# The order in which float64 weights are narrowed: blocks 4 to 7 of the first layer

## The chip, the cores and the metric

The kernel runs on one core of a Trainium2 chip. The metric is the device time in microseconds (us) of one execution, as the median of several runs. A separate profiled execution gives the trace from which durations are taken.

The core has five engines with a queue each: TensorE (PE in the profile; its weight loads are PEld), VectorE (DVE), ScalarE (ACT), GpSimd (POOL) and SyncE (SP, which here issues most of the transfers). Each engine works through its own queue in order and waits on semaphores for what other engines or transfers deliver.

## The reference

Two layers follow each other. The first is a state-space layer (Mamba2 SSD) over `x` of 4 x 8 x 768 x 32, computed in chunks of 32; its output, brought to 3072 tokens of 256 features, goes through a feed-forward block:

```python
h = x @ w_in                                # 3072 x 256 by 256 x 2048
g = h * (1.0 / (1.0 + np.exp(-1.702 * h)))  # quick GELU
return (g @ w_out).astype(np.float32)       # 2048 x 256
```

Inside a chunk the first layer needs decays `exp(cum_i - cum_j)`, a causal product of C and B weighted by them, and a state carried from chunk to chunk. The weights `w_in` and `w_out` come as float64.

## The kernel before

**Tiling.** The 3072 tokens are worked in 6 groups of 512. The 2048 hidden features are 16 blocks of 128 (f = 0 to 15), and each block's weights are two tiles of 128 x 128. For group 0 the hidden layer is a plain product: `hidden(0, f)` issues the matmuls of block f into a PSUM bank (line 895; TensorE's queue holds them as four matmul rows of 128 x 512 per block) and a SiLU on ScalarE (line 898). There are four such banks, used in turn, so block f needs block f-4's SiLU done. Later groups use a scheme with seven products in place of eight (`first`, `product`), with sums of blocks prepared on VectorE.

**Narrowing the weights.** The kernel loads the 64-bit words as pairs of 32-bit words and builds float32 from the fields. This goes in pieces (`PIECES`): pieces 0 to 3 hold two blocks of `w_in` each (0-1, 2-3, 4-5, 6-7), pieces 4 and 5 four blocks each (8-11, 12-15), and pieces 6 to 9 are `w_out`. For each piece:

- `fetch(i)` (line 180): SyncE issues two transfers.
- `fields(i)`, the first step (lines 192 and 195): VectorE cuts out the exponent (tile p) and the mantissa (tile m) of the high words.
- `clamp(i)` (lines 203 and 204): ScalarE turns the exponent field, in place, into that of a float32.
- `rounded(i)` (line 208): VectorE adds the low words to the mantissa.
- `join(i, parts)`, the last step (lines 222 and 228): VectorE puts the sign to the exponent and multiplies by the mantissa; the result is the piece's part of `w_in` or `w_out`. With `parts=2` it does this in two halves of the columns, each with its own two instructions, so that the first blocks are usable before the last. The joins of pieces 1 and 5 also issue a later fetch.

`narrow(i)` does `rounded(i)`, `join(i)` and `fields(i + 1)`, in an order that depends on i.

**Order.** The order on every engine is that of the program text (`in_order` at the end fixes it). For group 0 the loop over f runs `hidden(0, f)` and then what `in_hidden[0]` lists for that f:

```python
for i, k, c in ((2, 1, 1), (3, 2, 2), (4, 4, 7), (5, 8, 11), (6, 11, 14), (7, 14, 15)):
    at(in_hidden[0], k, lambda i=i: narrow(i))
    at(in_hidden[0], c, lambda i=i: clamp(i + 1))
```

So `narrow(2)` and the clamp of piece 3 come after block 1, `narrow(3)` and the clamp of piece 4 after block 2, `narrow(4)` after block 4, the clamp of piece 5 after block 7. `join(0, 2)`, `join(1)`, `fields(2)` and `clamp(2)` come before the loop.

**What else lies there.** After block 5, SyncE's queue holds the store of the decays, further fetches and loads. After block 8, `pick_a` (line 369, ScalarE) makes X from the clipped decays `az`; after block 9, `fan_all` (line 415, TensorE) spreads X over the partitions into ab, and VectorE scans it into the decays L (line 453). After block 15 group 0's second product starts (line 992, tiles o), with the narrowing of `w_out` beside it. Ahead of block 9 of that second product come the scores cb (line 685), the product A (line 716, `gain`), and CsT (line 670, `since_start`), which VectorE makes from the transposed C in the PSUM bank that A's second tile uses after it.

Of the kernel before, what the change touches and what calls it, by code (L numbers as in the profile page):

```python
# [35 lines left out]
def kernel(  # L36
# [126 lines left out]
    def fetch(i, held=False):  # L163
        name, f, n = PIECES[i]
        if n == 2 and f % 4:
            t = pieces.pop(i - 1)[:, 2 * n * DM:]
        else:
            t = pieces[i] = words(f"bits{i}")
            t = t[:, :2 * n * DM]
        if held:  # L170
            held.memset(t[:, :1], 0)
        if name == "in":
            src = moe_w_in[:, 2 * f * P:2 * (f + n) * P].rearrange("(k p) e -> p k e", p=P)
            dst, src = (v.rearrange(s, h=n, e=2 * P) for v, s in (
                (t, "p (h k e) -> k p h e"), (src, "p k (h e) -> k p h e")))
        else:
            src = moe_w_out[f * P:(f + n) * P, :].rearrange("(f p) (h e) -> h p f e", p=P, h=2)
            dst = t.rearrange("p (h f e) -> h p f e", h=2, f=n)
        for k in range(2):
            nc.sync.dma_start(out=dst[k], in_=src[k])  # L180
        t = t.rearrange("p (e w) -> p e w", w=2)
        bits[i] = t[:, :, 0], t[:, :, 1]
# [5 lines left out]
    def fields(i):  # L188
        hi, cols = bits[i][1], slice(0, PIECES[i][2] * DM)
        mantissa[i] = wide.tile([P, PN], U32, tag="m", name=f"m{i}")[:, cols]  # L190
        power[i] = wide.tile([P, PN], U32, tag="p2", name=f"p2{i}")[:, cols]
        nc.vector.tensor_scalar(out=power[i], in0=hi, scalar1=0x7FF00000, scalar2=None,
                                op0=ALU.bitwise_and)

        nc.vector.tensor_scalar(out=mantissa[i], in0=hi, scalar1=0x000FFFFF,
                                scalar2=0x00100000, op0=ALU.bitwise_and, op1=ALU.bitwise_or)
# [9 lines left out]
    def rounded(i):  # L206

        nc.vector.scalar_tensor_tensor(out=mantissa[i].bitcast(FP32), in0=bits[i][0],
                                       scalar=2.0 ** -32, in1=mantissa[i],
                                       op0=ALU.mult, op1=ALU.add)  # L210
# [4 lines left out]
    def join(i, parts=1):  # L215

        name, f, n = PIECES[i]
        n //= parts
        low, m, p2 = bits.pop(i)[1], mantissa.pop(i), power.pop(i)
        for k in range(parts):  # L220
            cols, fs = slice(k * n * DM, (k + 1) * n * DM), slice(f + k * n, f + (k + 1) * n)
            nc.vector.scalar_tensor_tensor(out=p2[:, cols], in0=low[:, cols], scalar=0x80000000,  # L222
                                           in1=p2[:, cols], op0=ALU.bitwise_and, op1=ALU.bitwise_or)
            if name == "in":
                dst, h = w_in[:, fs].rearrange("p f k e -> p (f k e)").unsqueeze(1), 1
            else:
                dst, h = w_out[:, :, fs].rearrange("p c f e -> p c (f e)"), 2
            nc.vector.scalar_tensor_tensor(  # L228
                out=dst, in0=m[:, cols].bitcast(FP32).rearrange("p (h e) -> p h e", h=h),
                scalar=2.0 ** -20, in1=p2[:, cols].bitcast(FP32).rearrange("p (h e) -> p h e", h=h),  # L230
                op0=ALU.mult, op1=ALU.mult)
        for n in NEXT.get(i, ()):
            fetch(n)

    def narrow(i):
        rounded(i)
        if i in (4, 5):
            join(i, 2)
        if i + 1 < len(PIECES):
            fields(i + 1)  # L240
        if i not in (4, 5):
            join(i)


    scratch = dram.tile([NC, 2, NB * NH, H], FP32, name="scratch")
# [989 lines left out]
# [3 lines that stand above are left out]
# [6 lines left out]
    at(in_project[0], 2, lambda: decay(PG + 1), lambda: clip_rows(1),  # L1244
       lambda: decay_rows(1), lambda: turn(PG + 1))
    at(in_project[0], 5, lambda: narrow(9))
    at(in_project[0], 9, lambda: score(pairs), lambda: gain(pairs), lambda: keep_both(pairs, True),
       lambda: weigh(PG), lambda: weigh(PG + 1))
# [201 lines left out]
```

## Time and profile before

| what | value |
|---|---|
| runs: median (lowest to highest) | 349.3 us (348.98 to 349.34) |
| profiled execution: its own time | 350.67 us |
| profiled execution: span from first to last instruction | 348.8 us |
| granted TensorE clock, mean | 1.000 |
| TensorE busy | 341.6 us |
| VectorE busy | 254.6 us |
| ScalarE busy | 155.0 us |
| HBM traffic over the span | 73 GB/s |

A row of the timeline has the start in us, the duration in us, engine, line, operation, tiles out<-in, shape, and the number of instructions merged in it; brackets at its end give idle time of that engine just before and what ended it. In a list of waits the three numbers are the total in us, the number of times, and the longest. Idle time of an engine that nobody waits for costs nothing. Ends of matmuls are modelled.

### The profile page before, as it was taken

Reading aid. Unit: us, or ns where it says so; the run is one execution under the profiler, and the core shown is the slowest. Engines: PE = TensorE matmul, PEld = TensorE weight load, DVE = VectorE, ACT = ScalarE, POOL = GpSimd, SP = SyncE. Lnnn points to the kernel's source line nnn. Section 1 sums busy time; section 2 is a strip of 40 time slices with the busy share of each in tenths; the row PEclk is TensorE's granted clock in tenths of the full one; section 3 lists DMA queues with packets and bytes.
Section 4 is the critical chain, followed back from the end, with each engine's and each line's share of the span. In section 5 each row is a group of like instructions: output and inputs, shape, how many; then the busy total and the mean of one; then the engine's idle time right before and its main releaser. Section 6 shows DMA issues by size and latency. Waiting matters only on the chain.

```text
span 348.8 us, 8124 instructions
## 1 busy us (share of the span) xinstructions
PE 341.6 (98%) x3380; PEld 268.9 (77%) x3380; DVE 254.6 (73%) x481; ACT 155.0 (44%) x352; POOL 13.1 (4%) x42
## 2 busy tenths in 40 slices
PE   8989999999999999999999999999999999999996
PEld 6634444445688888888888888888888888899996
DVE  5889997999878999667997467788465654465463
ACT  4797585205453322654432554332564331554320
POOL 8300000100000100000000000000000000000000
PEclk9999999999999999999999999999999999999999
DMA  6599889624627200415704027400000300000301
GB/s 158 134 300 213 189 181 245 113 54 105 113 49 131 66 0 2 75 57 124 123 18 63 0 59 130 73 1 2 0 4 3 55 7 0 0 2 0 62 0 61
DMA packets 89980, 25.92 MB, mean 74 GB/s; under 512 B 73432, under 2 KB 87128, under 8 KB 89944
## 3 DMA queue, kind: packets, MB, share of 16 engines
q1 hardware_dynamic: 89112, 24.88, 33.5%
q10 hardware_dynamic: 832, 0.52, 0.5%
q8 instruction: 26, 0.43, 0.5%
q14 instruction: 10, 0.08, 0.1%
HBM read 22.15 MB, written 3.24 MB: 73 GB/s over the span
## 4 chain that ended last, share of the span: by engine, by line
PE 90%; DMA 3%; DVE 2%; SPq 1%; ACT 1%; issue 1%; ACTq 1%; POOL 0%; DVEq 0%
PE acc L1055 28%; PE X L950 19%; PE Y L960 14%; PE o L992 8%; PE acc L1062 7%; PE h L895 5%; DMA bits<-in_moe_w_in_dram 3%; PE y L839 2%; PE cb L685 2%; PE y L825 1%; SPq L180 1%; PE A L716 1%; PE ab L557 1%; DMA zC<-in_C_dram 1%; DVE p L222 1%
## 5 line engine op out<-in xcount | busy, mean ns | idle before, releaser
L955 ACT ACTIVATE ac<-X 128x256 f32<-128x256 f32 x76 | 29.1, 383 | 81.5 <-PE X L950 80.7
L1082 DVE TENSOR_TENSOR gT<-Y,ac 128x512 f32<-128x512 f32 x38 | 26.2, 689 | 40.1 <-PE Y L960 32.5
L1055 PE MATMUL acc<-mg,mw 128*128 128x256 f32 x192 | 54.5, 379 | 0.0
L927 ACT ACTIVATE gT<-gT 128x512 f32<-128x512 f32 (+1 forms) x76 | 38.9, 518 | 29.0 <-DVE gT L1082 28.5
L950 PE MATMUL X<-my,mi 128*128 128x256 f32 x152 | 45.1, 380 | 0.0
L1055 PEld LDWEIGHTS acc<-mg,mw 128*128 128x128 f32 x192 | 36.5, 190 | 5.0
L895 PE MATMUL h<-yT,w_in 128*128 128x512 f32 x80 | 35.6, 598 | 1.1 <-DVE w_in L228 0.6
L1082 DVE TENSOR_TENSOR gT<-Y,b 128x256 f32<-128x256 f32 x38 | 15.9, 419 | 28.5 <-PE Y L960 28.5
L1055 PE MATMUL acc<-gT,w_out 128*128 128x256 f32 x128 | 35.5, 379 | 0.0
L950 PEld LDWEIGHTS X<-my,mi 128*128 128x128 f32 x152 | 28.0, 190 | 3.9 <-ACT ac L955 0.2
L895 PEld LDWEIGHTS h<-yT,w_in 128*128 128x128 f32 x80 | 14.7, 190 | 19.7 <-issue 15.9
L992 PE MATMUL o<-gT,w_out 128*128 128x512 f32 x64 | 28.3, 595 | 0.0
L918 DVE TENSOR_TENSOR mg<-gT 128x512 f32<-128x512 f32 x40 | 27.2, 681 | 0.0
L1055 PEld LDWEIGHTS acc<-gT,w_out 128*128 128x128 f32 x128 | 24.2, 190 | 3.4 <-ACT yT L873 0.2
L955 ACT ACTIVATE b<-X 128x256 f32<-128x256 f32 x38 | 14.6, 383 | 21.2 <-PE X L950 20.7
L950 PE MATMUL X<-yT,w_in 128*128 128x256 f32 x76 | 23.2, 389 | 0.0
L960 PE MATMUL Y<-yT,w_in 128*128 128x256 f32 x76 | 22.7, 381 | 0.0
L960 PE MATMUL Y<-my,mi 128*128 128x256 f32 x76 | 22.7, 380 | 0.0
L960 PE MATMUL Y<-yT,mi 128*128 128x256 f32 x76 | 22.5, 379 | 0.0
L950 PE MATMUL X<-my,w_in 128*128 128x256 f32 x76 | 22.5, 379 | 0.0
L992 PEld LDWEIGHTS o<-gT,w_out 128*128 128x128 f32 x64 | 11.8, 190 | 13.6 <-issue 13.4
L405 DVE TENSOR_TENSOR_SCAN L<-a,idents 128x1024 f32<-128x1024 f32 x9 | 20.5, 2277 | 0.2 <-DMA a<-scratch 0.2
(159 smaller groups left out, 546.9 us busy)
## 6 DMA issues: line engine op xcount, KB each, us to landing
a<-scratch SPq DMA_DIRECT2D x18, 256.0 KB, 4.8
bits<-in_moe_w_out_dram SPq DMA_DIRECT2D x8, 512.0 KB, 6.6
x<-in_x_dram SPq DMA_DIRECT2D x24, 128.0 KB, 3.1
out_dram<-ob SPq DMA_DIRECT2D x40, 64.0 KB, 1.9
bits<-in_moe_w_in_dram SPq DMA_DIRECT2D x8, 256.0 KB, 4.4
bits<-in_moe_w_in_dram SPq DMA_DIRECT2D x4, 512.0 KB, 11.9
b<-in_B_dram SPq DMA_DIRECT2D x20, 64.0 KB, 2.6
af<-in_a_dram SPq DMA_DIRECT2D x3, 384.0 KB
```

What stands on the lines that cost most here:

```text
L405: nc.vector.tensor_tensor_scan(out=L, data0=ra[p].rearrange("p k e -> p (k e)"), data1=idents.rearrange("p h i -> p (h i)"), initial=0.0, ...
L685: nc.tensor.matmul(out=s["cb"][side, r, k].rearrange("p (q i) -> p q i", q=Q), lhsT=BT[rows, k, side], rhs=CT[rows, k, :, side], start=Tru ...
L895: nc.tensor.matmul(out=h, lhsT=w_in[:, f, k], rhs=yT[g][:, k], start=(k == 0), stop=(k == NK - 1), skip_group_check=True)
L918: nc.vector.tensor_tensor(out=t[:, 0:2], in0=B[:, :, 1], in1=B[:, 0], op=ALU.subtract)
L927: nc.scalar.activation(o, i, AF.Silu, scale=GELU_SCALE)
L950: nc.tensor.matmul(out=s["X"], lhsT=lhsT, rhs=rhs, start=i == "1", stop=i == "4", skip_group_check=True)
L955: nc.scalar.activation(copy, s["X"], AF.Copy)
L960: nc.tensor.matmul(out=o, lhsT=lhsT, rhs=rhs, start=s.pop("new", False), stop=i != "5", skip_group_check=True)
L992: nc.tensor.matmul(out=o[c], lhsT=w_out[:, c, f], rhs=gT[g, f // 2][:, f % 2], start=(f == 0), stop=(f == NF - 1), skip_group_check=True)
L1055: nc.tensor.matmul(out=acc[g][0][i][:, cols], lhsT=w, rhs=h[:, cols], start=(j == 0 and k == 0 and (i, 0) in begins), stop=(j == NF // 2 - ...
L1062: nc.tensor.matmul(out=o[k] if type(o) is list else o[:, cols], lhsT=h[:, cols], rhs=w, start=(j == 0 and (i, k) in begins), stop=(j == NF ...
L1082: nc.vector.tensor_tensor(out=o, in0=v, in1=w, op=ALU.add)
```

## The change

Two things change in `narrow`. For piece 2 (blocks 4 and 5) the last step is put ahead of the first step on piece 3 (blocks 6 and 7). For piece 3 the last step stays behind the first step on piece 4, but works on one block at a time: two pairs of instructions on 256 columns each instead of one pair on 512.

```diff
     def narrow(i):
         rounded(i)
-        if i in (4, 5):
-            join(i, 2)
+        if i in (2, 4, 5):
+            join(i, 1 if i == 2 else 2)
         if i + 1 < len(PIECES):
             fields(i + 1)
-        if i not in (4, 5):
-            join(i)
+        if i not in (2, 4, 5):
+            join(i, 2 if i == 3 else 1)
```

On VectorE the queue from the rounding of piece 2 to the rounding of piece 4 becomes (before on the left):

```
rounded(2)             rounded(2)
fields(3)              join(2)            2 instructions, 128x512
join(2)                fields(3)
rounded(3)             rounded(3)
fields(4)              fields(4)
join(3)                join(3) block 6    2 instructions, 128x256
                       join(3) block 7    2 instructions, 128x256
rounded(4)             rounded(4)
```

The order on the other engines' queues is the same as before; VectorE has two instructions more.

## The prediction

> **What bounds the kernel now.** I read the page's first two parts, then PE's waits, then each engine's timeline between 15 and 68 us, where the weights are prepared. Page:
> ```profile
> span 348.8 us, 8124 instructions
> PE 341.6 (98%) x3380; PEld 268.9 (77%) x3380; DVE 254.6 (73%) x481; ACT 155.0 (44%) x352; POOL 13.1 (4%) x42
> ```
> PE is busy in 98% of the span. So a change off PE counts only where it moves one of PE's few idle stretches. PE's waits from 17 to 68.5 us (who, whom, total, times, longest):
> ```profile
> PE ab L415 <- ACT X L369: 0.8, 1, 0.8
> PE h L895 <- DVE w_in L228: 0.6, 1, 0.6
> PE A L716 <- DVE CsT L670: 0.3, 1, 0.3
> ```
> From 68.5 to 348 us the same view lists no wait at all: what comes after 68.5 us follows PE's own stream. The three waits in PE's timeline:
> ```profile
> 26.18 10.57 PE L895 MATMUL h<-yT,w_in 128*128 128x512 f32 x24 [0.63 <-DVE w_in L228]
> ...
> 37.59 0.69 PE L415 MATMUL ab<-X,ones 32*64 32x256 f32 x16 [0.84 <-ACT X L369]
> ...
> 67.53 0.70 PE L716 MATMUL A<-x,Be 64*32 64x64 f32 x47 [0.31 <-DVE CsT L670]
> ```
> The first is the matmul of block 4, held by the join of piece 2 (blocks 4, 5). The second is the fan-out of X, which ScalarE makes. The third is the gate that matters: everything later hangs on 67.53. VectorE:
> ```profile
> 17.02 0.42 DVE L222 SCALAR_TENSOR_TENSOR p<-bits,p 128x256 uint32<-128x256 uint32 x1
> 17.47 0.42 DVE L228 SCALAR_TENSOR_TENSOR w_in<-m,p 128x256 f32<-128x256 f32 x1
> ...
> 23.94 0.43 DVE L192 TENSOR_SCALAR p<-bits 128x512 uint32<-128x512 uint32 x1 [0.75 <-DMA bits<-in_moe_w_in_dram]
> ...
> 24.62 0.69 DVE L222 SCALAR_TENSOR_TENSOR p<-bits,p 128x512 uint32<-128x512 uint32 x1
> 25.34 0.69 DVE L228 SCALAR_TENSOR_TENSOR w_in<-m,p 128x512 f32<-128x512 f32 x1
> ...
> 26.87 0.69 DVE L192 TENSOR_SCALAR p<-bits 128x1024 uint32<-128x1024 uint32 x1 [0.24 <-DMA bits<-in_moe_w_in_dram]
> ...
> 28.80 0.69 DVE L228 SCALAR_TENSOR_TENSOR w_in<-m,p 128x512 f32<-128x512 f32 x1
> 29.41 1.22 DVE L208 SCALAR_TENSOR_TENSOR m<-bits,m 128x1024 f32<-128x1024 uint32 x1
> ...
> 33.21 0.69 DVE L192 TENSOR_SCALAR p<-bits 128x1024 uint32<-128x1024 uint32 x1
> ...
> 57.72 0.69 DVE L192 TENSOR_SCALAR p<-bits 128x1024 uint32<-128x1024 uint32 x1 [1.77 <-DMA bits<-in_moe_w_out_dram]
> ...
> 67.04 0.42 DVE L670 TENSOR_TENSOR CsT<-tp,since 128x256 f32<-128x256 f32 x1
> ```
> VectorE waits for transfers at 23.94, 26.87 and 57.72. The last wait is 1.77 long, and from there VectorE's chain of scans leads to CsT at 67.04, whose end releases A. So the gate hangs on a transfer, not on the steps that are moved. ScalarE:
> ```profile
> 25.89 0.58 ACT L898 ACTIVATE gT<-h 128x512 f32<-128x512 f32 x1
> 27.60 1.15 ACT L203 ACTIVATE p<-p,edge 128x1024 f32<-128x1024 uint32 x1 [1.14 <-DVE p L192]
> ...
> 33.93 1.15 ACT L203 ACTIVATE p<-p,edge 128x1024 f32<-128x1024 uint32 x1
> ```
> ScalarE has 1.14 us idle before the clamp of piece 4. The clamp of piece 5 starts 0.03 after VectorE's p (33.21 + 0.69 = 33.90): VectorE sets it.
>
> **The change, part by part.** Neither moved step issues a transfer (a join fetches only for pieces 1 and 5), and neither passes anything on SyncE's or GpSimd's queue; only VectorE's order changes.
>
> *Join of piece 2 first.* Its first instruction needs ScalarE's clamp of piece 2, whose second half runs 22.92 to 23.64. At 20.38 such an instruction started 0.04 after its clamp, so the join starts at 23.69 instead of 24.62. It takes 0.72 to the second instruction and 0.69 more: weights ready at 25.10, not 26.03. VectorE idled for the transfer until 23.94 anyway, so this new wait (0.5) costs nothing: its cover is that idle, 0.75. PE started 0.15 after the weights; 25.25 is earlier than PE's next free slot (26.18 less 0.63 idle less the 0.16 by which matmuls of 0.59 overlap at a pitch of 0.43: 25.39). Block 4 starts at 25.39, **0.79 earlier**, and the first wait is gone.
>
> *First step of piece 3 later.* Its p starts 0.61 after the join's last instruction, at 25.02, not 23.94: 1.08 later. Queued behind are m, rounding of piece 3 (25.81 to 26.50, before 25.95 to 26.64), and then piece 4's first step, which waits for its transfer until 26.87 as before. ScalarE waits for that p: clamp of piece 3 at 25.48 and 26.23, not 24.51 and 25.26; behind it the SiLU of block 2 moves from 25.89 to 26.86. ScalarE can start the next 0.48 later, at 27.34, before 27.60: the 1.14 idle hides it with 0.26 to spare. Without that cover it would cost up to 0.97.
>
> *Join of piece 3 in two halves.* The pair of 512 columns takes 28.09 to 29.41, 1.32. Pairs of 256, from the join of piece 0, go 16.22, 16.68, 17.02, 17.47, 17.81: 1.59 for both. So **VectorE loses 0.27**. Block 6 is ready at 28.97, not 29.50; block 7 at 29.76, 0.26 later, but PE needs it only at 30.84. PE reaches block 6 at 25.39 + 8 x 0.43 = 28.83, waits until 29.12, and runs blocks 6 to 9 some 0.53 earlier than before (29.65). Block 8's weights (31.96 + 0.27 + 0.15 = 32.38) still precede their slot at 32.56.
>
> The row says 0.27. [...]
>
> *What is late next.* Nothing on VectorE waits for a transfer between 26.87 and 33.21, so rounding and join of piece 4 and the first step of piece 5 all come 0.27 later: p at 33.48. ScalarE's clamp of piece 5 goes from 33.93 to 34.20, the SiLU of block 8 behind it to 36.43, X to 36.91, and the fan-out ab from 37.59 to 37.86. PE gets there 0.53 early and waits about 1.6 instead of 0.84. **The gain of 0.53 is eaten by the second wait, and PE leaves it 0.27 late.** From there PE runs without a gap to 66.92, so it comes to A 0.27 late. A waits for CsT, 0.31 before; 0.04 of that stays. VectorE's own 0.27 vanishes in its waits of 0.33 at 45.43 and 1.77 at 57.72. The transfer behind the latter was issued at 50.14 in a SyncE queue that waits for older transfers, not for these joins (its buffer is free at about 39).
>
> **Sum**: -0.79 (block 4) + 0.26 (block 6's new wait) + 0.53 (given back at ab) + 0.27 (ab later) - 0.27 (taken up at A) = **0.0 us** on the span of 348.8. The profiled execution took 350.67, 1.87 outside the span, unchanged. It lies 1.4 above the median of the runs, 349.3, to which I apply the 0.0: **349.3**. Bounds of the unknown: less than nothing only if PE's 0.53 survived both ab and A (-0.53); more if A's slack were missing (+0.27). I take 0, since 0.27 lies under 0.31, though narrowly.
>
> **The rivals.**
> *The delay goes through.* If in unprofiled runs the transfer for 57.72 lands earlier, A's wait is shorter and up to 0.27 shows: 349.6. For it: the runs are 1.4 shorter than the profiled one. Against: a DMA share of 0.99 from 50 to 57.6 us.
> *The gain goes through.* If ab were not set by VectorE's p and A not by CsT, 348.8. For it: removing a wait on the busiest engine. Against: 33.90 to 33.93, and 67.53. Both would have to be wrong.
> *Slower: the cover of the early join goes.* If the transfers for pieces 3 and 4 land early, the old order does piece 3's first step while the clamp of piece 2 runs (23.11 to 23.79), and loses nothing; the new one idles on VectorE from 23.11 to 23.69. Piece 4's first step could be at 25.73 in the old order and 26.42 in the new: 0.69, and 0.27 for the halves: 0.96, 350.3. It begins to count when piece 4's transfer lands before 26.4, and decides the sign at 0.2% when it lands about 0.45 before that and CsT's transfer early too. Against: DMA shares of 0.93 and 1.09 from 18 to 32 us.
> *Slower: PE's clock.* PE's idle stretch at ab doubles. The granted clock is 1.00 in every window, even 0 to 6 us with PE busy 4.64 of 6.00; from 32 to 38 it would now be busy about 4.4. Each matmul at twice its pitch would cost 0.43, so three of them pass 0.7: 350.5 or more. [...]
>
> **How the numbers follow.** No change 0.71; delay through 0.13; gain through 0.05; cover gone 0.09; clock 0.02. About 0.2% (0.7 us) is what a measurement of this kernel can tell from no change. The first two lie inside it and the third mostly; with scatter between runs (348.98 to 349.34 already) I give faster 0.05, same 0.84, slower 0.11. The range goes from the gain (348.8, less 0.1 scatter) to nearly the lost cover: 348.7 to 350.1.
>
> **What the profile after would show.** Right: no wait of h on w_in near 25.4; a wait of about 0.3 before block 6; ab near 37.86 after an idle of about 1.6; A still near 67.5 after almost none. Wrong: ab earlier than 37.5, ScalarE's clamp of piece 4 after 27.7, A moved, or a clock under 1.00.

## The result, and the profile after

The changed kernel takes 351.29 us (median of 20 runs, 349.66 to 352.87) against 349.19 us before (20 runs, 348.44 to 350.40). The ratio is 1.0051, with a 95% interval of 1.0036 to 1.0066: **slower by half a per cent**, about 1.8 us by the ratio (the medians lie 2.1 apart). The forecast was no change, 349.3 us, with a range up to 350.1. It was wrong.

The 20 runs after the change are of two kinds, by the TensorE clock that was granted. Nine have a mean clock of 0.999 or 1.000 and a median of 350.18 us; eleven have 0.994 or 0.995 and a median of 351.71 us. So there are two costs to explain: about 1.0 us in every run (0.8 in a second set of runs, below), and 1.5 us more in about half of them.

The profile shown here is of a run at 0.999 (349.66 us). The head of the page of the changed kernel, and TensorE's waits from 17 to 68.5 us:

```profile
span 347.7 us, 8127 instructions
PE 341.0 (98%) x3380; PEld 269.0 (77%) x3380; DVE 254.8 (73%) x483; ACT 155.0 (45%) x352; POOL 13.0 (4%) x42
```

```profile
PE ab L415 <- ACT X L369: 1.6, 1, 1.6
PE h L895 <- ACT yT L858: 0.5, 1, 0.5
```

Of the three waits that the prediction shows, two are gone: that for block 4 and that of A for CsT. The wait of 0.5 for yT is not new: the same view of the trace before has that line too, and the prediction's list leaves it out. The wait at ab has doubled, as forecast. But the span of this run is *shorter* than that of the trace the forecast was read from (348.8), while the changed kernel's runs are longer. So that trace did not show a usual execution. It took 350.67 us, and all 20 runs of the kernel before lie below that, as do 119 of the 126 made later. The kernel before was therefore profiled once more (first experiment); its waits over the same stretch:

```profile
PE ab L415 <- ACT X L369: 0.8, 1, 0.8
PE h L895 <- ACT yT L858: 0.5, 1, 0.5
```

In this usual execution (349.03 us, span 346.9) the old kernel does not wait for block 4 either, and A does not wait for CsT. The reason stands in VectorE's timeline. The kernel before, profiled again, from the first step of piece 2:

```profile
21.31 0.42 DVE L192 TENSOR_SCALAR p<-bits 128x512 uint32<-128x512 uint32 x1
...
22.11 0.69 DVE L208 SCALAR_TENSOR_TENSOR m<-bits,m 128x512 f32<-128x512 uint32 x1
22.71 0.43 DVE L192 TENSOR_SCALAR p<-bits 128x512 uint32<-128x512 uint32 x1
...
23.39 0.69 DVE L222 SCALAR_TENSOR_TENSOR p<-bits,p 128x512 uint32<-128x512 uint32 x1
...
25.34 0.70 DVE L192 TENSOR_SCALAR p<-bits 128x1024 uint32<-128x1024 uint32 x1
...
31.68 0.69 DVE L192 TENSOR_SCALAR p<-bits 128x1024 uint32<-128x1024 uint32 x1
```

The changed kernel:

```profile
21.18 0.42 DVE L192 TENSOR_SCALAR p<-bits 128x512 uint32<-128x512 uint32 x1
...
21.97 0.69 DVE L208 SCALAR_TENSOR_TENSOR m<-bits,m 128x512 f32<-128x512 uint32 x1
23.15 0.69 DVE L222 SCALAR_TENSOR_TENSOR p<-bits,p 128x512 uint32<-128x512 uint32 x1 [0.48 <-ACT p L204]
...
24.48 0.42 DVE L192 TENSOR_SCALAR p<-bits 128x512 uint32<-128x512 uint32 x1
...
25.89 0.72 DVE L192 TENSOR_SCALAR p<-bits 128x1024 uint32<-128x1024 uint32 x1
...
32.51 0.69 DVE L192 TENSOR_SCALAR p<-bits 128x1024 uint32<-128x1024 uint32 x1
```

None of these rows of the old order has idle time in front of it: the transfers of pieces 3 and 4 have landed. The same holds for all eleven traces made after the prediction with the transfers in their usual order: in none of them does VectorE wait for these two. Why they landed late in the one trace before, no run shows. With them there, the first step of piece 3 (22.71) fills just the time in which ScalarE clamps piece 2. In the new order the join of piece 2 stands there and waits 0.48 for that clamp with nothing beside it; the first step of piece 3 follows at 24.48. From the first step of piece 2 to that of piece 5 the old order takes 31.68 - 21.31 = 10.37 us, the new one 32.51 - 21.18 = 11.33.

### The profile page after: what moved, and what is told of

It reads as the page before. It is cut to its first block, busy times and chain, and to the rows that moved or that the text cites. A ratio compares the mean times of both kernels' runs of the same rounds, so it can differ in the third digit from the quotient of the medians.

```text
span 347.7 us, 8127 instructions
## 1 busy us (share of the span) xinstructions
PE 341.0 (98%) x3380; PEld 269.0 (77%) x3380; DVE 254.8 (73%) x483; ACT 155.0 (45%) x352; POOL 13.0 (4%) x42
## 4 chain that ended last, share of the span: by engine, by line
PE 91%; DMA 4%; SPq 3%; ACT 1%; issue 0%; POOL 0%; DVE 0%
PE acc L1055 28%; PE X L950 19%; PE Y L960 14%; PE o L992 8%; PE acc L1062 7%; PE h L895 5%; DMA bits<-in_moe_w_in_dram 3%; PE y L839 2%; PE cb L685 2%; SPq L180 2%; PE y L825 1%; PE A L716 1%; DMA c<-in_C_dram 1%; SPq L150 1%; PE busy L443 1%; PE ab L557 1%
```

## The experiments

Each kernel below was run in turn with the kernel before on the same chip. "Full clock" means a mean granted clock of 0.998 or more.

**1. Both kernels again.** No edit.

> The kernel before, unchanged, so that the granted clock and the span of each of its runs can be set beside those of the changed kernel, whose twenty runs fall into two kinds: clock 0.999 or 1.000 with spans of 347.7 to 348.4 us, and clock 0.994 or 0.995 with spans of 349.3 to 350.9. Clock theory (the wait of TensorE at ab, 1.6 us long after the change and 0.84 before it, brings the clock down in part of the executions): all runs of the kernel before at 0.999 to 1.000, median near 349.2. Rival (the clock falls in both kernels by chance and the change costs its time elsewhere): some of these runs at 0.995 too, about as many as after the change.

> The changed kernel, unchanged, on the same chip as the others of this set. Clock theory: part of the runs at clock 0.995, some 1.6 us longer than those at 1.000; those at 1.000 some 0.3 to 1.0 longer than the kernel before (the delay at ab goes through, because A does not wait for CsT). Rival: no split by clock, a shift of about 1.8 us in every run.

Before: 12 runs, all at full clock, median 349.26 us; of the 35 further runs of it in this set one was at 0.995 (352.05), and the other 34 have a median of 349.3. After: 12 runs, eight at full clock with a median of 350.09, four at 0.994 or 0.995 with a median of 351.56; the ratio of all is 1.0030 (1.0010 to 1.0051). Over all sets the kernel before was at reduced clock in 1 of 126 runs whose clock is listed, the changed kernel in 15 of 32. So the reduced clock belongs to the change, and besides it a constant 0.8 us in this set and 1.0 in the first. The profile of the changed kernel in this set caught a run at 0.994. TensorE's timeline there, and the windows of 1 us behind ab (columns: window, its length, busy time with count of PE, PEld, DVE, ACT and POOL, granted clock, share of the DMA engines, GB/s):

```profile
37.00 0.69 PE L415 MATMUL ab<-X,ones 32*64 32x256 f32 x16 [1.57 <-ACT X L369]
```

```profile
37.00:38.00 1.00, 1.00 (x18) 0.58 (x19) 0.96 (x3) 0.43 (x1) 0.00 (x0) 1.00 0.74 124
38.00:39.00 1.00, 1.00 (x5) 0.95 (x4) 1.00 (x2) 0.00 (x0) 0.00 (x0) 0.58 0.78 262
39.00:40.00 1.00, 1.00 (x2) 0.34 (x1) 1.00 (x3) 0.00 (x0) 0.00 (x0) 0.50 1.04 355
40.00:41.00 1.00, 1.00 (x2) 0.34 (x1) 1.00 (x3) 0.00 (x0) 0.00 (x0) 0.50 1.03 314
41.00:42.00 1.00, 1.00 (x3) 0.51 (x2) 1.00 (x2) 0.00 (x0) 0.00 (x0) 0.71 1.01 335
42.00:43.00 1.00, 1.00 (x3) 0.40 (x3) 0.93 (x5) 0.60 (x1) 0.00 (x0) 1.00 1.10 384
```

A fall to one half begins about 1.2 us after the end of the idle stretch (0.58 in the window from 38 is full clock to about 38.2 and half from there on). The lost clock adds up to 0.42 + 0.50 + 0.50 + 0.29 = 1.71 us. From the start of ab to that of A it is 29.32 or 29.33 us in every trace at full clock that has the fan-out at its place, and 30.97 here: about 1.65 more.

**2. Each part alone.**

```diff
# early join alone
-            join(i, 2 if i == 3 else 1)
+            join(i)
# halves alone (against the kernel before)
-            join(i)
+            join(i, 2 if i == 3 else 1)
```

> Only the first part of the change: the join of piece 2 ahead of the first step of piece 3; the join of piece 3 whole. Clock theory: VectorE loses nothing, so ab comes when it came before, but TensorE comes to it up to 0.5 us earlier and waits about 1.3 instead of 0.84; the time of runs at full clock is that of the kernel before within 0.2 us, and a smaller part of the runs than with the whole change, perhaps none, is at 0.995. Theory that the halved join costs all: no difference from the kernel before in anything.

> Only the second part: the join of piece 3 one block at a time, the old order kept. Clock theory: VectorE is 0.27 us later from there on, ab 0.27 later, TensorE waits about 1.1 there and 0.6 before block 4; the clock stays at 1.000 in most runs, and the time is 0.0 to 0.3 us above the kernel before. Theory that the halved join costs all: the same 1.8 us as the whole change.

The early join alone: 349.67 us, none of 12 runs at reduced clock. The halves alone: 349.56 at full clock, one of 12 reduced. Neither ratio to the kernel before can be told from 1 (1.0006 and 0.9999, both within about 0.002), so the medians alone would not carry the split; the traces do. In microseconds, from the starts of the rows:

| trace | first step of piece 2 to 4 | piece 4 to 5 | piece 5 to ab | sum | idle at ab |
|---|---|---|---|---|---|
| before, as forecast from (transfers late) | 5.16 | 6.34 | 4.38 | 15.88 | 0.84 |
| before again | 4.03 | 6.34 | 4.59 | 14.96 | 0.75 |
| early join alone | 4.70 | 6.32 | 4.38 | 15.40 | 0.84 |
| halves alone | 4.14 | 6.59 | 4.39 | 15.12 | 0.91 |
| whole change | 4.71 | 6.62 | 4.39 | 15.72 | 1.58 |
| whole change again | 4.70 | 6.61 | 4.39 | 15.70 | 1.57 |

Each row is one trace. The early join costs VectorE 0.67. Of this 0.48 is the wait; 0.08 more is lost because the waiting join does not start, as its neighbours do, some 0.08 before the end of the instruction in front; and about 0.1 because the rounding of piece 3 now stands right behind the m that it needs: in the changed kernel it starts 0.04 after that m ends (at 25.28, behind 24.82 + 0.42), in the kernel before, profiled again, 0.08 before the end of the join in front of it (at 24.72, before 24.11 + 0.69). The halves cost 0.25 to 0.30 between pieces 4 and 5. (The halves' 4.14 is 0.11 above the 4.03, ahead of the step that was edited: so far do two traces differ.) Whatever the delay, its first 0.2 is taken up on ScalarE, for in the old order the SiLU of block 7, not VectorE, holds back the clamp of piece 5 (4.59 against 4.39). VectorE's p ends there at 31.68 + 0.69 = 32.37, and the clamp starts at 32.62, behind the SiLU:

```profile
32.12 0.60 ACT L898 ACTIVATE gT<-h 128x512 f32<-128x512 f32 x1 [1.12 <-PE h L895]
32.62 1.14 ACT L203 ACTIVATE p<-p,edge 128x1024 f32<-128x1024 uint32 x1
```

So ab comes 0.16 later with the halves, 0.44 later with the early join, and **0.74 to 0.76 later with both**; the single delays add up to less because each has lost that 0.2. My expectation that the early join alone would leave ab where it was fell, and the idle times at ab of 1.3 and 1.1 that I expected of the two parts were 0.84 and 0.91.

**3. The idle stretch filled, in the changed kernel.**

```diff
+    at(in_hidden[0], 9, lambda: dense(8, area("filler")[:, 0]))
     at(in_hidden[0], 9, lambda: fan_all(PG))
```

> The changed kernel with one extra matmul row pair of 128x512 on constants (0.86 us of TensorE, its result read by nobody) put behind block 9, into the idle stretch before ab. Clock theory: the idle stretch falls from 1.57 to about 0.7, as in the kernel before; no run at 0.995, all at 0.999 or 1.000, and the median is that of the changed kernel's full-clock runs, 350.0 to 350.2 us, about 0.9 above the kernel before. If the falls have another cause, a third to a half of the runs stay at 0.995, and the median is 350.3 or more.

The wait at ab falls to 0.67, and **none of 12 runs is at reduced clock**. The median is 350.43 us, ratio 1.0023 (1.0010 to 1.0036) to the kernel before; the constant cost stays. The median lies 0.2 to 0.3 above what was expected for it, and 1.0 above the 349.40 of the kernel before in its own set, where 0.9 was expected; the interval is too wide to call that a further cost. The trace has one wait of 0.2 us at 119 us that neither trace of the changed kernel has.

**4. The idle stretch made longer, in the kernel before.** Two ScalarE copies ahead of X; in a second kernel only one.

```diff
+    at(in_hidden[0], 8, lambda: nc.scalar.activation(cum, cum, AF.Copy),
+       lambda: nc.scalar.activation(cum, cum, AF.Copy))
     at(in_hidden[0], 8, lambda: pick_a(PG))
```

> The kernel before, old order, with two ScalarE copies of 128x256 in place (about 0.8 us, on data that is not needed any more) ahead of the two that make X, so that TensorE waits about 1.55 us at ab without anything changed on VectorE. Clock theory: a third to a half of the runs at 0.995, those 1.6 us longer; the full-clock runs at about 350.1 us, 0.8 above the kernel before. If the falls come from the new order of the joins rather than from the idle stretch, all runs at full clock.

> The kernel before with one copy of 128x256 on ScalarE ahead of X, not two: TensorE waits about 1.15 us at ab. Clock theory: between the kernel before (0.75, 1 run in 47 at 0.995) and two copies (1.5, 6 of 12): 1 to 3 of 12 at 0.995; full-clock runs 0.4 above the kernel before.

With two copies TensorE waits 1.51 at ab, and 6 of 12 runs are at reduced clock, median 351.65; the other six have 350.07, 0.7 above the kernel before in this set (349.40), where ab starts 0.78 later in the trace. This is the changed kernel's picture with VectorE's order untouched, so the new order of the joins is not needed for the clock to fall: the longer idle stretch is enough. With one copy:

```profile
36.47 0.69 PE L415 MATMUL ab<-X,ones 32*64 32x256 f32 x16 [1.05 <-ACT X L369]
```

The execution profiled here kept its full clock. Five of 12 runs are reduced (350.86), more than I expected; the other seven have 349.43, 0.2 above the kernel before, where I expected 0.4 (ab starts 0.2 later). Kernels with an idle stretch of 0.75 to 0.91 in their traces have reduced clocks in 3 of 162 runs (the kernel before 1 of 126, the early join 0 of 12, the halves 1 of 12, the old order of experiment 5 without filler 1 of 12). So it begins to be frequent somewhere about 1 us; 1 of 12 at 0.91 against 5 of 12 at 1.05 are too few runs to say where.

**5. Late transfers in both orders.** The loads of `a` (`rows_a(az, ...)`) are queued ahead of the transfers of pieces 3 to 5; then the same with the filler of experiment 3.

```diff
-    for i in range(2, 6):
-        fetch(i)
+    fetch(2)
     rows_a(az, (nc.sync,))
+    for i in range(3, 6):
+        fetch(i)
```

> The kernel before with the loads of the decays a queued on SyncE ahead of the transfers of pieces 3, 4 and 5, so that these land later and VectorE waits for them, as in the trace that the prediction was read from. Theory that the cover decides (the old order fills the wait for the clamp with the first step of piece 3, if its transfer has landed): the old order loses some 0.5 to 1.0 us before piece 4; TensorE waits for block 4 again; time 349.5 to 350.5.

> The changed kernel with the same late transfers; to be compared with the old order with late transfers. Theory that the cover decides: where piece 4's transfer holds VectorE in both, the new order comes to ab only 0.27 later, not 0.94, so that the full-clock runs differ by about 0.3 us; runs at 0.995 remain, as the idle stretch at ab is still about 1.5. Rival (the new order costs 0.9 whatever the transfers do): full-clock runs 0.9 us above the old order with late transfers.

> The old order with the late transfers of the earlier pair (loads of a ahead of pieces 3 to 5), and with the extra matmul of 0.86 us on constants behind block 9, so that the clock does not fall and the two orders can be compared at full clock. About 350.5 us, as with late transfers alone, no run at 0.995.

> The new order with the same late transfers and the same extra matmul. Theory that the cover decides: VectorE waits for piece 4's transfer in both orders, so the new order is 0.3 us slower than the old one (the halved join alone). Rival: 0.9 us slower, as with early transfers.

Without the filler: the old order 350.47 us in 11 runs at full clock and one at 0.995 (353.50); the new one had only one of 6 runs at full clock (350.53), the other five at 351.9 to 355.22. I had expected TensorE to wait for block 4 again in the old order; in its trace it does not. With the filler: 350.1 (12 runs) and 350.9 (6 runs), a difference of 0.8, nearer to the rival's 0.9 than to my 0.3. The medians do not settle the question, because the lateness could not be held: piece 4's transfer kept VectorE waiting 1.44 and 1.45 us in two of the four traces, 0.54 in one and not at all in the last one, the new order with filler. Where it did hold VectorE, a part of the forecast's arithmetic is seen. The first steps of pieces 4 and 5, old order with late transfers and filler:

```profile
27.04 0.69 DVE L192 TENSOR_SCALAR p<-bits 128x1024 uint32<-128x1024 uint32 x1 [1.45 <-DMA bits<-in_moe_w_in_dram]
33.39 0.69 DVE L192 TENSOR_SCALAR p<-bits 128x1024 uint32<-128x1024 uint32 x1
```

New order with late transfers:

```profile
27.51 0.69 DVE L192 TENSOR_SCALAR p<-bits 128x1024 uint32<-128x1024 uint32 x1 [1.44 <-DMA bits<-in_moe_w_in_dram]
34.11 0.69 DVE L192 TENSOR_SCALAR p<-bits 128x1024 uint32<-128x1024 uint32 x1
```

In the new order, too, VectorE had done all in front 1.44 us before the transfer landed, so the early join's 0.67 was covered there; from piece 4 on it is 6.35 and 6.60, and the new order loses only the halves' 0.25. That the two landings (27.04 and 27.51) would be the same in both orders is not shown, and no pair of medians at full clock shows the cover. The trace of the new order without the filler is the run of 355.22 us, with a mean clock of 0.990: behind idle stretches of 1.11 us (for weights) and 1.64 us (at ab) its half clock lasts from about 39.4 to 46.2 us, twice as long as in experiment 1.

**6. X on GpSimd, in the kernel before.**

```diff
-            nc.scalar.activation(X[:, :, q], az[:, c:c + 2], AF.Copy, scale=pick[:, b, q:q + 1])
+            nc.gpsimd.tensor_scalar(out=X[:, :, q], in0=az[:, c:c + 2], scalar1=pick[:, b, q:q + 1],
+                                    scalar2=None, op0=ALU.mult)
```

> The kernel before with X made on GpSimd, which is idle there, in place of ScalarE, so that ab no longer stands behind the clamp of piece 5. If ab is what sets the time: two GpSimd multiplications of 128x256 at about 0.73 each after the clipped a (33.8 in the repeated trace) end near 35.3, ab starts up to 0.75 earlier, at 35.5, the wait there is gone, and the time is 0.5 to 0.75 us below the kernel before, 348.6 to 348.9. If something later takes it back (A's wait for CsT), no difference.

Slower: 350.91 us, ratio 1.0068 (1.0037 to 1.0100), with 5 of 10 runs at reduced clock. The other five have 349.89, where I had expected 348.6 to 348.9. GpSimd's two instructions (1.83 and 0.91, in a profile whose spans on GpSimd are rough) are longer than the 0.73 that I took for one from its rows of CsT; merged in one row:

```profile
34.27 2.73 POOL L369 TENSOR_SCALAR X<-az,pick 128x256 f32<-128x256 f32 x2 [21.62 <-DMA c<-in_C_dram]
```

TensorE waits 1.17 at ab for it in that trace, whose clock is full, and the clock falls in as many runs as in experiment 4; two of the five are at 0.990.

**7. The fan-out one block later, in both orders.**

```diff
-    at(in_hidden[0], 9, lambda: fan_all(PG))
-    at(in_hidden[0], 9, since_fanned)
+    at(in_hidden[0], 10, lambda: fan_all(PG))
+    at(in_hidden[0], 10, since_fanned)
```

> The kernel before with the fan-out of X (ab, and what VectorE makes of it) put behind block 10 instead of block 9, so that TensorE works on block 10 (1.72 us) while X is made. If the wait at ab (0.75) is all that TensorE loses here, it is gone and the time is 0.5 to 0.75 us below the kernel before; no run at 0.995. If VectorE's lateness itself sets the time further on (through A's wait for CsT), no difference.

> The changed kernel with the fan-out of X behind block 10. Theory that everything the change costs, the delay of 0.9 and the clock, comes in through the wait at ab (1.57): that wait is gone, X at 36.95 coming just before the new slot at 37.15; no run at 0.995; the time falls from 350.1 (full clock) and 351.7 (reduced) to between 348.5 and 348.9, the same as the old order with the fan-out behind block 10 within 0.4. Rival (VectorE's 0.94 us matter elsewhere too, at A): 0.4 to 0.9 above the old order with the same fan-out.

TensorE works on block 10 while X is made, and the wait at ab is gone in both. The old order: 349.12 us (11 runs at full clock, median 349.09, and one at 0.99 whose place no trace shows), ratio 0.9994 (0.9973 to 1.0015), no gain that can be told from none. The new order: 349.60, all 12 at full clock, ratio 1.0005 (0.9991 to 1.0019), so against the kernel before the changed kernel's slowness is gone within what can be measured. Neither reached the 348.5 to 348.9 that I expected. Where a part of the 0.75 of the old order went stands in TensorE's waits, old order first, then the new one:

```profile
PE h L895 <- ACT yT L858: 0.5, 1, 0.5
PE A L716 <- DVE CsT L670: 0.4, 1, 0.4
```

```profile
PE o L992 <- DVE w_out L228: 0.5, 1, 0.5
PE h L895 <- ACT yT L858: 0.5, 1, 0.5
```

In these two traces TensorE, which no longer waits at ab, waits for VectorE later: 0.4 at A in one, 0.5 at the second layer's weights in the other. The wait at A hangs on a transfer, as in the trace before: VectorE had waited 1.38 us for a piece of `w_out` there. The two orders differ by 0.5 in the medians at full clock. That lies in the rival's range (0.4 to 0.9), but runs scatter over nearly 2 us or more in each, so whether VectorE's lateness counts further on stays open. No version here beats the kernel before.

## Why the prediction was wrong

**The step that failed** is the cover of the early join: "this new wait (0.5) costs nothing: its cover is that idle, 0.75". The size of the wait was right (0.48 measured). The cover was a wait for a transfer that the one traced execution had and none of the eleven later traces with the usual order of transfers has. What fills the wait for the clamp in usual executions of the old order is the first step of piece 3; with the join ahead of it nothing did, and VectorE came to piece 4 later by 0.67 us. With it fell the statement that piece 4's first step waits for its transfer "until 26.87 as before". The prediction noticed that its profiled execution was 1.4 us longer than the runs, and still applied the difference worked out in it to their median.

**The rival that held** was "the cover of the early join goes". Its 0.69 for the lost cover was 0.67, its 0.96 for both parts 0.94 and 0.96 on VectorE, and its 350.3 the 350.1 and 350.2 of the runs at full clock; 0.2 of VectorE's delay did not reach ab, which it had not seen. It had a chance of 0.09.

**The absorption at A** failed for the same reason. A's wait of 0.31 hung on the transfer behind 57.72 in that trace. In the traces made since with the fan-out at its place, A does not wait for CsT. In the changed kernel CsT ends 1.3 us before A starts:

```profile
64.49 0.42 DVE L670 TENSOR_TENSOR CsT<-tp,since 128x256 f32<-128x256 f32 x1
...
66.22 0.79 PE L716 MATMUL A<-x,Be 64*32 64x64 f32 x56
```

So what ab loses goes through, and the 0.27 "taken up at A" had nothing there to take it up. Delaying ab with copies in the old order (experiment 4) shows the same: 0.78 later at ab, 0.7 at the end.

**The clock** was listed as a rival with a chance of 0.02: I took an idle stretch of about 1.6 us to be too short for the clock to fall, which no run shows. The "twice its pitch" of that rival was not shown by any trace then either; the windows of experiment 1 show it, 2 matmuls in a window of 1 us at a clock of 0.50, against 3 or 4 at 1.00 from 39 to 43 us in the first trace of the changed kernel. The fall came in 15 of 32 runs and gives nearly half of the loss. Added up: 0.74 at ab, and 15/32 of 1.5 to 1.7 (0.7 to 0.8), is 1.4 to 1.5 us; the ratio says 1.3 to 2.3. The runs at full clock lost 0.8 and 1.0 where the traces show 0.74 to 0.76 at ab; the rest is not explained.

In two traces the clock fell to 0.50, for some 3.4 us by windows of 1 us, behind idle stretches of 1.57 and 1.51 us, and it fell in 5 of 12 runs of a kernel whose trace has one of 1.05. The trace that the forecast was read from has 0.84 there, and a clock of 1.00 in every window.

**What was right.** The 0.27 for the halves (0.25 to 0.30); and clamp, SiLU and X behind VectorE's p, as two rows of ScalarE in the changed kernel show:

```profile
33.23 1.15 ACT L203 ACTIVATE p<-p,edge 128x1024 f32<-128x1024 uint32 x1 [0.71 <-DVE p L192]
...
35.95 0.90 ACT L369 ACTIVATE X<-az,pick 128x256 f32<-128x256 f32 x2
```

**What was right by luck.** The idle time of about 1.6 at ab (1.58) came by another way. The forecast added 0.53 by which TensorE would be early to 0.27 by which ab would be late. In usual executions TensorE waits for block 4 in neither order, so the terms -0.79 and +0.26 of the sum had nothing to act on (the second is 29.12 - 28.83 = 0.29 by the forecast's own rows): counted from the first step of piece 2, TensorE comes to ab after 14.2 us in the old order and 14.1 in the new, and nearly all of the 0.8 is ab being late. For the same reason the wait for block 4 was not removed by the change, and the wait forecast before block 6 did not come. ScalarE's clamp of piece 4 before 27.7 (26.80) says nothing either: the old order has it at 26.07. Three of the signs that the forecast had named for being wrong did come: ab before 37.5 (36.90), A moved (66.22), and a clock under 1.00. The first two say little of the change, since the kernel before, profiled again, has 36.27 and 65.60.

## What to carry to other kernels

Before a wait in a trace is used as cover, ask whether usual executions have it: a profiled run that is longer than the other runs of its kernel may show waits that are not the rule, as it did here, and a difference worked out in it should not be applied to the median before a second trace has shown the same waits. Work put ahead of a wait on another engine needs something behind it that is always there; here the first step of the next piece was that work. And an idle stretch on TensorE that grows from 0.75 to a little over 1 us may cost more by the clock than by its length: with one copy (experiment 4) 0.2 us in the runs at full clock, and 1.4 on top of it in the 5 of 12 at reduced clock. So it is worth listing the granted clock of many runs and not of one.

## What the runs showed of the hardware that was not expected

- TensorE's clock fell to 0.50 for about 3.4 us behind an idle stretch of 1.57 and of 1.51 us in two traces, and for about 6.8 us behind one of 1.11 and one of 1.64 in a third. One fall of 3.4 us costs 1.65 us between ab and A. Counted in runs by the mean clock, with the stretch taken from the one trace of each kernel: 1 of 126 at 0.75, 1 of 24 at 0.84, 1 of 12 at 0.91, 5 of 12 at 1.05, 5 of 10 at 1.17, 21 of 44 at 1.51 to 1.58, 5 of 6 at 1.64. From 1.05 to 1.58 the length hardly changes how often it happens.
- Filling some 0.9 us of such a stretch with matmuls on constants that nobody reads stopped the falls (0 of 12 runs, against 15 of 32).
- On GpSimd a multiplication of 128x256 by a scalar per partition took 1.83 and 0.91 us for two alike in a row, against 0.74 for its product of two tensors of that size in the trace of before; spans on GpSimd are rough in these profiles.
